# One shared block for four engines' loops, a branch hint marked in every turn, an evener spread of q, and a shorter early part of wo

## The chip, the cores and the metric

One core of one Trainium2 chip. The time is device microseconds (us) of one execution; times of a kernel are medians of several executions, with the lowest and highest where they matter. The profile is one such execution, and its span, from the first to the last instruction, is 1.3 to 1.6 us shorter than the time of the same run. No execution of any kernel was over 1.5% above the fastest of the same kernel, so all count as fast.

## The reference

One decode step of attention with grouped heads, gated by a small MLP. All tensors are bf16.

```python
def _A_ref(x, k_cache, v_cache, wq, wo):          # k_cache, v_cache: [2, 8, 32768, 128]
    q = (x @ wq).reshape(B, Sq, Hq, Dh).transpose(0, 2, 1, 3)      # Hq = 32, Dh = 128
    k = jnp.repeat(k_cache, rep, axis=1)                            # rep = 4
    v = jnp.repeat(v_cache, rep, axis=1)
    p = _softmax(jnp.einsum("bhqd,bhkd->bhqk", q, k) * (Dh ** -0.5), axis=-1)
    o = jnp.einsum("bhqk,bhkd->bhqd", p, v)
    return o.transpose(0, 2, 1, 3).reshape(B, Sq, Hq * Dh) @ wo
...
x = A_x                                            # [2, 1, 512]
xn = _layernorm(x, axis=-1)
s = _A_ref(xn, A_k_cache, A_v_cache, A_wq, A_wo)
g = _silu(_B_ref(xn, B_w1, B_w2, B_w3, B_w4))      # the MLP, 512 -> 512 -> 1792 -> 512
return x + s * g
```

There are 2 x 8 = 16 head groups, each with 8.39 MB of K and 8.39 MB of V, read once.

## The kernel before

SyncE issues all large loads in order. Each of the other engines runs a loop over the head groups, and they hand work on through semaphores. The parts that the change and the argument touch, with cuts marked:

```python
WO_PARTS = [(0, 0, 8), (0, 8, 16), (1, 0, 8), (1, 8, 12), (1, 12, 14), (1, 14, 15), (1, 15, 16)]
...
hint_p, hint_v = pe.mark_branch_hint_location(), dve.mark_branch_hint_location()   # at the program's start
...
wait(pool, k_qT, (g_, g_.n))                       # q is spread by 16 casts of GpSimd
for n in range(NQ):
    for j in range(NQ):
        G(spread(pool, j, n))
...
with act.Fori(0, NG):                              # NG = 16: ScalarE, exp of the scores
    ...
with pool.Fori(0, NG) as m:                        # GpSimd, places q for the next group
    ...
with dve.Fori(0, NG // 2) as t:                    # VectorE, two groups in a turn
    for odd in range(2):
        heads(oA[:, bass.ds(t * (2 * RS) + odd * RS, RS)], 0)   # closes the group before
        group(odd)                                              # transposes K, then the exponentials
...                                                # VectorE: copies and heads() of the last group
turn = pe.alloc_register("turn")                   # TensorE
pe.reg_mov(turn, 0)
nc.br("turn", engines=[pe.engine])
nc.switch_bb("turn")
loop = nc.cur_bb
head_sums()
pe.reg_add(turn, turn, 1)
pe.br_lt(turn, NG + 1, on_true="group", on_false="tail")
nc.switch_bb("group")
...                                                # the K and V products of one group
nc.br("turn", engines=[pe.engine])
nc.switch_bb("tail", parent=loop)
...                                                # the wo product; output by SyncE
sp.wait_ge(s_out, 16)
...
for eng, hint, reg in ((pe, hint_p, turn), (dve, hint_v, end)):
    eng.br_lt(reg, 1, on_true="more", on_false="end").branch_hint(hint)
nc.switch_bb("more")
pe.sem_inc(s_end, 1)
dve.sem_inc(s_end, 1)
nc.switch_bb("end", parent=tail)
```

The last branches are never taken. They exist so that a hint can be attached to them. In the program a hint names a branch that comes later. The trace has TensorE's hint once, at 1.53 us, for 0.04 us.

The softmax here doesn't subtract the row's maximum and nothing guards it: scores larger than these inputs give would overflow.

## Time and profile before

| | kernel before |
|---|---|
| time, median of 3 | 653.87 us (653.72 to 654.01) |
| span of the profiled run | 652.4 us |
| bytes read | 280.50 MB |
| DMA in the loop (52 to 610 us) | 434 GB/s, share 1.00 |
| busy: TensorE / VectorE | 58% / 58% |
| last row of wo landed | 649.43 us |
| output issued, end of span | 650.68, 652.42 us |

The time is that of one uninterrupted stream of loads, with about 3 us behind the last byte. The prediction shows the lines. Two views of the kernel before that it didn't show became important. The first is what SyncE waits for at the end (engine, line, what it waited for: us in total, times, longest):

```profile
SPq L648 <- DMA out_dram<-out: 1.0, 1, 1.0
```

The second is the time line where VectorE enters its loop (start, duration, instruction, and in brackets the idle time before it with its releaser):

```profile
37.15 0.68 DVE L427 TENSOR_TENSOR g_f<-T 32x512 f32<-32x512 f32 x1 [0.69 <-ACT T L425]
38.46 0.69 DVE L502 TENSOR_TENSOR ox<-ps,sel_t 128x512 f32<-128x512 f32 x1 [0.63 <-DVEq L46]
```

VectorE's first multiply inside the loop starts 0.63 us after its last instruction ahead of the loop.

### The profile page before, as it was taken

How to read it: one execution, taken by the hardware profiler on the slowest of the kernel's cores; microseconds unless marked ns; L12 is line 12 of the kernel's file. 1: busy time of each engine (PE TensorE's matmuls, PEld its weight loads, DVE VectorE, ACT ScalarE, POOL GpSimd, SP SyncE). 2: the span in 40 equal slices, each digit the busy share in tenths (PEclk: the TensorE clock that was granted, in tenths of full speed). 3: DMA queues.
4: the chain of work that ended last, by engine and by line, in shares of the span. 5: the costliest groups of instructions: out<-in, count | busy, mean ns of one | idle time of the engine just before them, and what ended most of it. 6: DMA issues, size and time to landing. Idle time of an engine off the chain costs nothing. (4 is left out here: it accounts for less than half of the span.)

```text
span 652.4 us, 6348 instructions
## 1 busy us (share of the span) xinstructions
PE 376.6 (58%) x2164; PEld 140.1 (21%) x2196; DVE 375.5 (58%) x430; ACT 49.4 (8%) x92; POOL 11.9 (2%) x45
## 2 busy tenths in 40 slices
PE   0758392673829458283854819376381946728674
PEld 0213131221213122021321203122130312203221
DVE  6368392754729365481945639285472927548671
ACT  1011010000101001010100101000010100101010
POOL 1200000000000000000000000000000000000000
PEclk9859688785978968597786969769596886959797
DMA  9989998999899989998999899989998999899997
GB/s 387 482 386 450 450 450 386 450 450 450 386 450 450 446 390 450 450 450 386 450 450 450 386 450 450 450 386 450 450 450 386 450 450 450 386 450 420 447 420 322
DMA packets 6509, 280.51 MB, mean 430 GB/s; under 512 B 746, under 2 KB 1004, under 8 KB 1260
## 3 DMA queue, kind: packets, MB, share of 16 engines
q1 hardware_dynamic: 6492, 280.50, 99.5%
q14 instruction: 1, 0.01, 0.0%
q10 hardware_dynamic: 16, 0.00, 0.0%
HBM read 280.50 MB, written 0.00 MB: 430 GB/s over the span
## 5 line engine op out<-in xcount | busy, mean ns | idle before, releaser
L566 PE MATMUL ps<-T,zeros 128*128 128x512 bf16 x992 | 276.5, 425 | 173.2 <-PEq L46 164.4
L486 DVE STREAM_TRANSPOSE T<-kbuf 128x1024 int32<-128x1024 int32 x256 | 291.2, 1207 | 116.5 <-DVEq L46 115.7
L566 PEld LDWEIGHTS ps<-T,zeros 128*128 128x128 bf16 x1024 | 98.8, 104 | 346.1 <-issue 267.8
L579 PE MATMUL ps<-vbuf,pt 128*16 128x512 bf16 x1024 | 71.3, 441 | 40.5 <-PEq L46 40.5
L502 DVE TENSOR_TENSOR ox<-ps,sel_t 128x512 f32<-128x512 f32 x17 | 11.8, 692 | 83.4 <-DVEq L46 83.4
L453 ACT ACT_TABLE_LOAD x16 | 20.5, 1283 | 445.5 <-ACTq L46 445.5
L579 PEld LDWEIGHTS ps<-vbuf,pt 128*16 128x16 bf16 x1024 | 29.8, 101 | 82.1 <-issue 65.2
L493 DVE STREAM_TRANSPOSE pt<-ep 128x512 bf16<-128x512 bf16 x32 | 22.1, 692 | 28.7 <-DVEq L46 28.7
L543 PE MATMUL ps<-ob,sel_h 128*128 128x129 f32 x34 | 9.0, 350 | 39.3 <-PEq L46 39.3
L453 ACT ACTIVATE ep<-ps 128x512 bf16<-128x512 f32 x32 | 19.1, 597 | 104.7 <-ACTq L46 104.5
L507 DVE TENSOR_REDUCE ob<-ox 128x128 f32<-128x512 f32 x17 | 17.3, 1018 | 2.5
L543 PEld LDWEIGHTS ps<-ob,sel_h 128*128 128x128 f32 x34 | 5.8, 212 | 47.5 <-issue 47.5
L463 POOL TENSOR_TENSOR zeros<-qr,sel_j 128x64 bf16<-128x64 f32 x16 | 4.7, 294 | 571.8 <-POOLq L46 571.8
L343 PE MATMUL ps<-kbuf,xT 128*2 128x512 bf16 x32 | 3.6, 623 | 15.1 <-DVE xT L300 15.1
L511 DVE RECIPROCAL rec<-ps 128x1 f32<-128x1 f32 (+1 forms) x17 | 2.9, 169 | 14.0 <-DVEq L46 14.0
L519 DVE TENSOR_REDUCE oA<-xm 128x128 f32 x16 | 5.9, 366 | 3.8 <-DVEq L46 3.8
L417 PE MATMUL ps<-vbuf,zeros 128*32 x12 | 7.0, 585 | 0.8 <-issue 0.3
L513 DVE SCALAR_TENSOR_TENSOR xm<-ps,rec,mask 128x128 f32<-128x128 f32 (+1 forms) x17 | 6.0, 351 | 2.5
L453 ACT ACTIVATION_READ_ACCUMULATOR ep<-ps 128x1 f32 x32 | 6.2, 194 | 0.0
L423 DVE TENSOR_TENSOR T<-T,ps 32x512 f32<-32x512 f32 x1 | 0.7, 674 | 8.7 <-PE ps L421 8.7
L359 POOL CAST qr<-qT 32x64 bf16<-32x64 f32 x16 | 4.6, 286 | 4.9 <-DVE qT L352 4.0
L343 PEld LDWEIGHTS ps<-kbuf,xT 128*2 128x2 bf16 x32 | 0.9, 113 | 16.8 <-DVE xT L300 15.1
(59 smaller groups left out, 45.1 us busy)
## 6 DMA issues: line engine op xcount, KB each, us to landing
vbuf<-in_A_v_cache_dram SPq DMA_DIRECT2D x4, 4096.0 KB, 26.1
kbuf<-in_A_k_cache_dram SPq DMA_DIRECT2D x2, 4096.0 KB, 22.4
kbuf<-in_A_wq_dram SPq DMA_DIRECT2D x1, 4096.0 KB, 12.3
vbuf<-in_B_w_dram SPq DMA_DIRECT2D x2, 1792.0 KB, 17.1
kbuf<-in_A_wo_dram SPq DMA_DIRECT2D x3, 1024.0 KB, 32.3
kbuf<-in_A_wo_dram SPq DMA_DIRECT2D x1, 512.0 KB, 35.0
kbuf<-in_A_wo_dram SPq DMA_DIRECT2D x1, 256.0 KB, 35.2
kbuf<-in_A_wo_dram SPq DMA_DIRECT2D x2, 128.0 KB, 35.0
```

The source lines that it names most:

```text
L417: pe.matmul(h2[0:32, :], lhsT=h_bf[:, bass.ds(f, 1), :].rearrange("p f c -> p (f c)"), rhs=w4v[:, bass.ds(f, 1), :].rearrange("p f d -> p ...
L453: act.activation(out=eps_[i][:, :], in_=sc[i][:, :], func=ACT.Exp, scale=inv_sqrt_dh, accum_out=rss[i][:, :]).then_inc(s_e, 1)
L463: pool.tensor_tensor(out=zw, in0=qr[:, :, :, bass.ds(m * rep, rep)].rearrange("p n e h -> p (n e) h").unsqueeze(2).to_broadcast([128, NB * ...
L486: dve.transpose(out=Ts[(NR * i + r) % T_BUFS][:, :].rearrange("p (b t k) -> p t b k", b=NB, t=RT), in_=kt[:, r * W:(r + 1) * W].rearrange( ...
L493: dve.transpose(out=pts[h][:, :, :].rearrange("p r (t h) -> p t r h", h=rep), in_=eps_[i][:, :].rearrange("p (t r h) -> p t r h", r=NR, h= ...
L502: dve.tensor_tensor(out=ox[:, :].rearrange("p (t d) -> p t d", t=VT), in0=o[:, :].rearrange("p (t d) -> p t d", t=VT), in1=sel_t[:, :].uns ...
L507: dve.tensor_reduce(out=ob[:, 0:Dh], in_=ox[:, :].rearrange("p (t d) -> p d t", t=VT), axis=AX.X, op=ALU.add).then_inc(s_ob, 1)
L513: dve.scalar_tensor_tensor(out=xm[p0:, :, :], in0=oT[p0:, 0:Dh].rearrange("p (w r) -> p w r", w=WL), scalar=rec[p0:, 0:1], in1=mask[p0:, : ...
L519: dve.tensor_reduce(out=dst, in_=xm[p0:, :, :].rearrange("p w r -> p r w"), axis=AX.X, op=ALU.add).then_inc(s_r, 1)
L543: mm = pe.matmul(oT, lhsT=sel_h[:, :, :, :].rearrange("p j h w -> p (j h w)"), rhs=ob[:, :], start=True, stop=True)
L566: mm = pe.matmul(sc2[:, bass.ds(i * 512, 512)], lhsT=z[:, nb, e, zc:zc + 128], rhs=Tb[:, nb, :, e], start=(r == 0 and nb == 0 and e == 0), ...
L579: mm = pe.matmul(o[32 * j:32 * j + VT * rep, :], lhsT=pts[h][:, r, a * VT * rep:(a + 1) * VT * rep], rhs=vt[:, u * VT:(u + 1) * VT, :].rea ...
```

## The change

It has four parts. (1) The loops of ScalarE, GpSimd, VectorE and TensorE no longer have blocks of their own: all four begin at one label, "turn". (2) TensorE's hint isn't marked at the start for a branch at the end any more; it is marked at the head of each turn, for the loop's own compare-and-branch, which replaces the unconditional one. (3) Six of GpSimd's sixteen casts that spread q go to VectorE (4) and ScalarE (2). (4) The early partial sums of wo end at row 11 and not at row 12. The intent is that the hint goes with the branch that is taken in every turn, and that the end gets a little shorter. Cut to its core (VectorE's closing statements, which only move behind TensorE's loop in the text, are left out):

```diff
-WO_PARTS = [(0, 0, 8), (0, 8, 16), (1, 0, 8), (1, 8, 12), (1, 12, 14), (1, 14, 15), (1, 15, 16)]
+WO_PARTS = [(0, 0, 8), (0, 8, 16), (1, 0, 8), (1, 8, 11), (1, 11, 14), (1, 14, 15), (1, 15, 16)]
...
-    hint_p, hint_v = pe.mark_branch_hint_location(), dve.mark_branch_hint_location()
+    hint_v = dve.mark_branch_hint_location()
...
+    wait(act, k_qT)
     wait(pool, k_qT, (g_, g_.n))
+    wait(dve, k_qT)
     for n in range(NQ):
         for j in range(NQ):
-            G(spread(pool, j, n))
+            if n == 0:
+                V(spread(dve, j, n))
+            elif n == 1 and j < 2:
+                A(spread(act, j, n))
+            else:
+                G(spread(pool, j, n))
...
-    with act.Fori(0, NG):
+    turn = {e: e.alloc_register("turn") for e in (pe, act, pool, dve)}
+    for e in turn:
+        e.reg_mov(turn[e], 0)
+    nc.br("turn", engines=[e.engine for e in turn])
+    nc.switch_bb("turn")
+    loop = nc.cur_bb
+
+    @contextmanager
+    def turns(e, n):
+        yield e.snap(turn[e], min_val=0, max_val=n - 1)
+        e.reg_add(turn[e], turn[e], 1)
+        e.br_lt(turn[e], n, on_true="turn", on_false="group")
+
+    with turns(act, NG):
...
-    with pool.Fori(0, NG) as m:
+    with turns(pool, NG) as m:
...
-    with dve.Fori(0, NG // 2) as t:
+    with turns(dve, NG // 2) as t:
...
-    turn = pe.alloc_register("turn")
-    pe.reg_mov(turn, 0)
-    nc.br("turn", engines=[pe.engine])
-    nc.switch_bb("turn")
-    loop = nc.cur_bb
+    hint_p = pe.mark_branch_hint_location()
     head_sums()
...
-    nc.br("turn", engines=[pe.engine])
+    pe.br_lt(turn[pe], NG + 1, on_true="turn", on_false="tail").branch_hint(hint_p)
     nc.switch_bb("tail", parent=loop)
...
-    for eng, hint, reg in ((pe, hint_p, turn), (dve, hint_v, end)):
-        eng.br_lt(reg, 1, on_true="more", on_false="end").branch_hint(hint)
+    dve.br_lt(end, 1, on_true="more", on_false="end").branch_hint(hint_v)
     nc.switch_bb("more")
-    pe.sem_inc(s_end, 1)
     dve.sem_inc(s_end, 1)
```

More of the change, by code (lines that the diff above doesn't have):

```diff
@@ L1 @@
-from contextlib import ExitStack
+from contextlib import ExitStack, contextmanager
 import concourse.bass as bass
@@ L358, in spread @@
     def spread(eng, j, n):
-        return eng.tensor_copy(
+        return (eng.copy if eng is act else eng.tensor_copy)(
             out=qr[32 * j:32 * j + 32, :, :, :].rearrange("p a e (m n h) -> p (a e) m n h", n=NQ, h=rep)[
@@ L443 @@
         d_wo[i].after(sp.dma_start(out=wo3[:, g, w], in_=wos[:, g, w]), 16)
-    with act.Fori(0, NG):
+    wait(pool, (g_, g_.n), (v_, v_.n), (a_, a_.n))
+    pool.sem_inc(s_zf, 1)
+    wait(dve, (v_, v_.n), (g_, g_.n), k_x4)
+    dve.sem_inc(s_o, 1)
+    dve.sem_inc(s_tf, T_BUFS - 1)
+    dve.sem_inc(s_tl, 1)
+    turn = {e: e.alloc_register("turn") for e in (pe, act, pool, dve)}
[10 more added lines that the diff above has]
+    with turns(act, NG):
         for i in range(NPART):
@@ L458 @@
     zw = z[:, :, :, (NR - 1) * rep:].rearrange("p n e (j w) -> p (n e) j w", j=NQ)[:, :, :, 0:rep]
-    wait(pool, (g_, g_.n), (v_, v_.n), (a_, a_.n))
-    pool.sem_inc(s_zf, 1)
-    with pool.Fori(0, NG) as m:
+    with turns(pool, NG) as m:
         take(pool, s_zf)
@@ L521, in heads @@
             ).then_inc(s_r, 1)
-    wait(dve, (v_, v_.n), (g_, g_.n), k_x4)
-    dve.sem_inc(s_o, 1)
-    dve.sem_inc(s_tf, T_BUFS - 1)
-    dve.sem_inc(s_tl, 1)
-    with dve.Fori(0, NG // 2) as t:
+    with turns(dve, NG // 2) as t:
         for odd in range(2):
@@ L530 @@
             group(odd)
-    oA4 = oA[:, RS:].rearrange("p (b s j r) -> p j (b s) r", b=B, s=NS, j=NQ)
-    oX4 = oX[:, :].rearrange("p (s r) -> p s r", r=RS)
-    for j in range(NQ):
-        n = B * NS if j < NQ - 1 else B * NS - 1
-        w = slice(32 * j, 32 * j + 32)
-        i_c = dve.tensor_copy(out=oX4[w, 0:n, :], in_=oA4[w, j, 0:n, :])
-    i_c.then_inc(s_r, 1)
-    heads(oX4[32 * (NQ - 1):, B * NS - 1, :], 32 * (NQ - 1))
     def head_sums():
@@ L546, in head_sums @@
         mm.then_inc(s_x, 1)
-    turn = pe.alloc_register("turn")
-    pe.reg_mov(turn, 0)
-    nc.br("turn", engines=[pe.engine])
-    nc.switch_bb("turn")
-    loop = nc.cur_bb
+    hint_p = pe.mark_branch_hint_location()
     head_sums()
-    pe.reg_add(turn, turn, 1)
-    pe.br_lt(turn, NG + 1, on_true="group", on_false="tail")
+    pe.reg_add(turn[pe], turn[pe], 1)
+    pe.br_lt(turn[pe], NG + 1, on_true="group", on_false="tail")
     nc.switch_bb("group")
@@ L586 @@
     mm.then_inc(s_o, 1)
-    nc.br("turn", engines=[pe.engine])
+    pe.br_lt(turn[pe], NG + 1, on_true="turn", on_false="tail").branch_hint(hint_p)
     nc.switch_bb("tail", parent=loop)
+    oA4 = oA[:, RS:].rearrange("p (b s j r) -> p j (b s) r", b=B, s=NS, j=NQ)
+    oX4 = oX[:, :].rearrange("p (s r) -> p s r", r=RS)
+    for j in range(NQ):
+        n = B * NS if j < NQ - 1 else B * NS - 1
+        w = slice(32 * j, 32 * j + 32)
+        i_c = dve.tensor_copy(out=oX4[w, 0:n, :], in_=oA4[w, j, 0:n, :])
+    i_c.then_inc(s_r, 1)
+    heads(oX4[32 * (NQ - 1):, B * NS - 1, :], 32 * (NQ - 1))
     step = NS * RS // BS
@@ L648 @@
     sp.wait_ge(s_out, 16)
-    tail, s_end = nc.cur_bb, nc.alloc_semaphore("s_end")
-    end = dve.alloc_register("end")
+    tail, end, s_end = nc.cur_bb, dve.alloc_register("end"), nc.alloc_semaphore("s_end")
     dve.reg_mov(end, 1)
-    for eng, hint, reg in ((pe, hint_p, turn), (dve, hint_v, end)):
-        eng.br_lt(reg, 1, on_true="more", on_false="end").branch_hint(hint)
+    dve.br_lt(end, 1, on_true="more", on_false="end").branch_hint(hint_v)
     nc.switch_bb("more")
-    pe.sem_inc(s_end, 1)
     dve.sem_inc(s_end, 1)
```

## The prediction

> **What bounds the kernel now.** I read the page's table of DMA queues first, then a table of stretches, then the waits, then the end of the program in order of time. The queues come first because the kernel has only 280.5 MB to bring in and the engines' shares are low (TensorE and VectorE 58% each).
>
> ```profile
> q1 hardware_dynamic: 6492, 280.50, 99.5%
> q14 instruction: 1, 0.01, 0.0%
> HBM read 280.50 MB, written 0.00 MB: 430 GB/s over the span
> ```
>
> The columns of the first two lines are packets, MB and share of 16 engines' span. The data queue is busy for all of the span but its very ends, and exactly one packet of instructions was fetched while the kernel ran. Next the stretches: the loop, the last head group with the first rows of wo, and what follows the last byte of wo.
>
> ```profile
> core 0: us, PE busy (x) PEld busy (x) DVE busy (x) ACT busy (x) POOL busy (x), PEclk, DMA share, GB/s
> 52.00:610.00 558.00, 324.93 (x1896) 122.41 (x1923) 321.92 (x351) 39.89 (x75) 4.41 (x15) 0.80 1.00 434
> ...
> 640.00:649.10 9.10, 6.83 (x70) 2.23 (x62) 2.61 (x5) 0.27 (x1) 0.00 (x0) 0.69 0.96 394
> 649.10:652.40 3.30, 0.62 (x20) 0.35 (x16) 0.58 (x2) 0.31 (x1) 0.00 (x0) 1.00 0.00 1
> ```
>
> In the loop DMA runs at share 1.00 and 434 GB/s while every compute engine has 40% of its time free. (The digits 386 and 450 that alternate on the page are packets falling into slices; stretches of hundreds of us give 434.) The waits say the same from VectorE's side:
>
> ```profile
> DVE T L486 <- DVEq L46: 115.7, 15, 9.4
> ```
>
> That is us in total, times, longest. VectorE, which begins each head group by transposing K, waits 115.7/15 = 7.7 us in every turn after the first, until K has landed. The loads themselves are ahead: one 8.39 MB load takes 8.39 MB / 434 GB/s = 19.3 us, and the page has a median of 27.2 us from issue to landing of K, so a load stands 7.9 us in the queue before its bytes move. Both numbers say that a turn of the loop has about 7.7 us of slack. So only the two ends can move the time: about 1 us ahead of the first packet, and what follows the landing of wo. That end, in order of time:
>
> ```profile
> 648.16 0.10 PEld L604 LDWEIGHTS ps<-kbuf,zeros 128*17 128x17 bf16 x4 [0.85 <-DMA kbuf<-in_A_wo_dram]
> 648.17 0.61 PE L604 MATMUL ps<-kbuf,zeros 128*17 128x512 bf16 x4
> 648.80 0.12 PEld L616 LDWEIGHTS ps<-kbuf,zeros 128*17 128x17 bf16 x8 [0.53 <-DMA kbuf<-in_A_wo_dram]
> 648.80 0.40 PE L616 MATMUL ps<-kbuf,zeros 128*17 128x128 bf16 x8
> 648.83 0.59 ACT L629 COPY T<-ps 128x512 f32<-128x512 f32 x1 [16.95 <-PE ps L604]
> 649.46 0.13 PEld L633 LDWEIGHTS ps<-T,zeros 128*17 128x17 f32 x8 [0.54 <-ACT T L629]
> 649.47 0.41 PE L633 MATMUL ps<-T,zeros 128*17 128x128 f32 x8 [0.27 <-ACT T L629]
> ```
>
> Each line is start, duration, instruction, and in brackets the idle time before it with what ended it. The last four rows of the early sums (L604, rows 8 to 11 of the second half of wo) waited for DMA. ScalarE's copy of the sums followed at once, and TensorE sat idle 0.27 us before it could add the copied sums (L633). Products of rows 14 and 15 (8 matmuls, L616), two VectorE instructions of 0.29 us and the output transfer close the program.
>
> [...]The trace shows no such stall in this loop: one instruction packet in 652 us, and TensorE's first weight load of a new turn (L543, at 570.46) stands 0.12 us after the VectorE reduce that it waits for (569.32 + 1.02 = 570.34). [...]the four of L604 took 0.61 us together, and their median alone is 0.631 us.
>
> **The change part by part.**
>
> *One block for the loops of ScalarE, GpSimd, VectorE and TensorE.* Comparing the built programs, the instructions within each engine's loop are the same in number and order, apart from TensorE's. Loop counters and branches are as many. Nothing is on the path: 0 us.
>
> *TensorE's hint and branch.* Out: one hint at the program's start, a never-taken branch at its very end, an unconditional branch per turn. In: one hint per turn and a compare-and-branch in place of the unconditional one. [...]In each turn it lies where TensorE waits for two VectorE operations (0.69 + 1.02 us), so it is hidden even from the turn, and the turn has 7.7 us spare: 0 us. In the last turn, too, the hint runs while TensorE waits for the last reduce.
>
> *Spreading q.* Six of GpSimd's sixteen casts (0.286 us each, L359) move: four to VectorE, two to ScalarE. GpSimd is done 1.7 us earlier (near 23.6 us instead of 25.3), but its next instruction (L463) starts at 39.78 because it waits for other engines' counts. VectorE has 3.20 us idle from 19.76 before L388; four casts at an estimated 0.3 us fit. ScalarE is idle for 12.64 us there. 0 us.
>
> *Partial sums end at row 11.* Parts of 4 and 2 rows become 3 and 3. A row is 128 KB, so the fourth part ends 131072 B / 434 GB/s = 0.30 us earlier. From the issue times (613.08, 613.55, 614.02, 614.50) plus 35.0, 35.2, 35.1 and 34.9 us the parts land at 648.1, 648.75, 649.1 and 649.4; the fourth will land at 647.8. TensorE must also be free: batches of four 512-column matmuls at half clock (0.50 there) start about 0.43 us apart, and the previous one starts at 647.56, so the last batch of early sums can start at 648.0 instead of 648.17. Being three side by side and not four, it still takes 0.61 us. The copy then runs from about 648.65 to 649.24 instead of 648.83 to 649.42. The fifth part, now rows 11 to 13, lands at 648.75 as before, but has 12 matmuls: 8 took 0.40 us, of which one batch of four is about 0.13, so 12 take about 0.53: 648.80 to 649.33. Now TensorE, not the copy, is what the 8 matmuls of L633 wait for: 649.33 instead of 649.47. The last products need row 15, at 649.4; they come at about 649.45 to 649.55, just behind it. Gain: 0.14 us.
>
> Sum: 653.87 - 0.14 = 653.73 us; I say 653.7.
>
> **The rivals.**
>
> 1. *The hint now does harm at the exit.* [...]the code behind the loop is reached by a taken branch at the end of the last turn[...]. If that code must be fetched behind the full data queue, the stall lies wholly on the end. For the size: a 2 KB transfer issued on the ScalarE queue at 1.96 us landed at 8.2 us, so up to 6 us, giving 655 to 660. For it: the old hint stood there for something. Against: [...]before the change the exit showed 0.07 us (645.49 to 645.56).
>
> 2. [...]
>
> 3. *The gain of the row cut vanishes.* If the landing of row 15 or the matmuls of the longer fifth part end up last, the 0.14 us shrink to 0: 653.9. Or TensorE is back at full clock earlier and it becomes 0.3: 653.55.
>
> 4. *A stall per turn.* Anything below 7.7 us per turn is absorbed by the slack; only above that would it reach the time, 16-fold. Nothing points to it.
>
> **Range and chances.** The three runs of before lie 0.29 us apart, and the end offers at most the time between row 15's landing (649.4) and the end of the last product (650.0), 0.6 us: low 653.2. The upper end takes in rival 2 in part and the spread: 654.3. Rival 1 gets some 5% and remains within 2% (13 us) anyway. A gain of 13 us would need fewer bytes or more than 434 GB/s: chance 0.005. A loss of 13 us would need a stall of 8.5 us (7.7 + 13/16) in each turn: 0.01.
>
> **What would show each step right or wrong.** Right: 434 GB/s in the loop, VectorE's wait for K still near 7.7 us per turn, one instruction packet or so, the copy of the sums starting about 0.2 us earlier relative to the landing of the last rows, and no idle of TensorE before L633's counterpart. Wrong: more instruction packets than a few, a gap of over 0.3 us between the last head-sum matmul and the first wo product, a wait of the K transposes that has shrunk by microseconds, or an idle before the last products put down to the wo transfer. The time itself would refute me if it left 653.2 to 654.3, most likely upward through the exit.

The step of TensorE's hint stood at 0 us, and the sum is 653.87 - 0.14 = 653.73 us, with the row cut as its only term that isn't 0. 0 us stands as the author's estimate; the records of the kernel after have 0.04 us for a hint and 0.21 us for the branch, beside the 0.69 + 1.02 us that TensorE waits in each turn. "No such stall" in the text is a stall of TensorE at the loop's own branch. The 0.3 us for a cast on VectorE is an estimate; its four took 1.14 us together in the kernel after, 0.26 us each.

## The result, and the profile after

| | before | after |
|---|---|---|
| median, 6 runs each, same chip | 653.94 us (653.6 to 654.79) | 654.73 us (654.57 to 654.88) |
| span of the profiled run | 652.42 us | 653.54 us |
| last row of wo landed | 649.43 us | 649.76 us |
| from there to the issue of the output | 1.25 us | 1.37 us |
| from the issue of the output to the end | 1.74 us | 2.41 us |

The ratio is 1.001, with a 95% interval of 0.9998 to 1.0023. The interval takes in 1, so the times of this batch alone don't show that the kernel became slower; the spans further below do. Here and below a ratio is the mean time of one kernel's fast runs over that of the other's of the same rounds, so it is not quite the ratio of the medians quoted. "Within 2%" was right. The time is 1.0 us above the predicted 653.7 and 0.4 us above the upper end of the range.

The last three rows of the table add up the difference of the spans: 0.33 + 0.12 + 0.67 = 1.12 us. So the stream ended later, and the output took longer. The table of queues of the kernel after says what was in the way (packets, MB, share):

```profile
q1 hardware_dynamic: 6492, 280.50, 99.3%
q14 instruction: 2, 0.02, 0.0%
...
HBM read 280.50 MB, written 0.00 MB: 429 GB/s over the span
```

The same 6492 data packets and 280.50 MB, but two instruction packets instead of one, and a slightly lower share of the data queue. In the stretches (columns as in the prediction) the loop is what it was:

```profile
52.00:610.00 558.00, 330.12 (x1928) 121.35 (x1925) 321.90 (x349) 39.87 (x75) 4.38 (x15) 0.80 1.00 434
640.00:649.10 9.10, 6.49 (x61) 1.98 (x61) 2.61 (x5) 0.14 (x1) 0.00 (x0) 0.70 0.98 406
649.10:652.40 3.30, 1.31 (x28) 0.69 (x28) 0.58 (x2) 0.45 (x1) 0.00 (x0) 0.50 0.02 6
```

434 GB/s again; what changed is in the last stretch, where 6 GB/s now move instead of 1. VectorE's wait for K is unchanged too:

```profile
DVE T L511 <- DVEq L46: 115.4, 16, 9.3
```

It was 115.7 us. So no stall per turn has appeared. Looking at the transfers of 650 to 655 us alone, first in the kernel before, then in the kernel after:

```profile
DMA packets 12, 0.00 MB, mean 0 GB/s; under 512 B 12, under 2 KB 12, under 8 KB 12
...
q1 hardware_dynamic: 12, 0.00, 0.2%
```

```profile
DMA packets 13, 0.01 MB, mean 2 GB/s; under 512 B 12, under 2 KB 12, under 8 KB 12
...
q14 instruction: 1, 0.01, 0.6%
```

The twelve packets are the output. In the kernel after an instruction packet lies among them. The DMA records of the trace put it at 652.12 us, with 8192 bytes and 495 ns; nine of the output's packets lie at 652.40 to 652.45 us, the other three at 652.61 to 652.64 us, just behind it. In the kernel before all twelve lie at 651.96 to 652.04 us. SyncE's wait shows the effect:

```profile
SPq L666 <- DMA out_dram<-out: 1.7, 1, 1.7
```

1.7 us for 1.0 us. The other packet is at 41.89 us (8192 bytes, 309 ns), where the stream already runs. The packet of the kernel before was at 606.00 us and is gone. The end of the program in order of time, to be held against the seven lines in the prediction:

```profile
647.46 1.46 PE L622 MATMUL ps<-kbuf,zeros 128*17 128x512 bf16 x11 [0.20 <-DVE zeros L544]
...
648.96 0.58 ACT L647 COPY T<-ps 128x512 f32<-128x512 f32 x1 [16.86 <-PE ps L622]
...
649.13 0.50 PE L634 MATMUL ps<-kbuf,zeros 128*17 128x128 bf16 x12 [0.21 <-DMA kbuf<-in_A_wo_dram]
649.60 0.15 PEld L651 LDWEIGHTS ps<-T,zeros 128*17 128x17 f32 x8 [0.25 <-ACT T L647]
649.60 0.63 PE L651 MATMUL ps<-T,zeros 128*17 128x128 f32 x8
...
650.01 0.44 PE L634 MATMUL ps<-kbuf,zeros 128*17 128x128 bf16 x8
650.49 0.29 DVE L659 TENSOR_TENSOR sg<-ps,g 113x128 f32<-113x128 f32 x1 [3.08 <-PE ps L634]
```

TensorE adds the copied sums (L651) with no idle time before it, where it had been idle for 0.27 us. The copy starts 0.80 us ahead of the landing of the last row (649.76 - 648.96); it had been 0.60 us (649.43 - 648.83).

One more difference stood at the entry of VectorE's loop:

```profile
36.04 0.68 DVE L434 TENSOR_TENSOR g_f<-T 32x512 f32<-32x512 f32 x1 [0.69 <-ACT T L432]
38.37 0.69 DVE L527 TENSOR_TENSOR ox<-ps,sel_t 128x512 f32<-128x512 f32 x1 [1.64 <-DVEq L46]
```

The idle time is 1.64 us and no longer 0.63. Nothing waits for those 1.0 us, since the stream sets the pace (434 GB/s, share 1.00), but they are a mark.

### The profile page after: what moved, and what is told of

Its sections match the earlier page's. It is cut to its first block, busy times and chain, and to the rows that moved or that the text cites. A ratio compares the mean times of both kernels' runs of the same rounds, so it can differ in the third digit from the quotient of the medians.

```text
span 653.5 us, 6401 instructions
## 1 busy us (share of the span) xinstructions
PE 382.5 (59%) x2199; PEld 138.5 (21%) x2199; DVE 376.5 (58%) x434; ACT 50.0 (8%) x94; POOL 10.2 (2%) x39
## 3 DMA queue, kind: packets, MB, share of 16 engines
q1 hardware_dynamic: 6492, 280.50, 99.3%
HBM read 280.50 MB, written 0.00 MB: 429 GB/s over the span
## 5 line engine op out<-in xcount | busy, mean ns | idle before, releaser
L574 PE MATMUL ps<-T,zeros 128*128 128x512 bf16 x1024 | 280.5, 424 | 168.5 <-PEq L46 163.5
L511 DVE STREAM_TRANSPOSE T<-kbuf 128x1024 int32<-128x1024 int32 x256 | 291.3, 1207 | 115.8 <-DVEq L46 115.4
L587 PE MATMUL ps<-vbuf,pt 128*16 128x512 bf16 x1024 | 74.6, 456 | 38.8 <-PEq L46 38.8
L269 DVE MEMSET ps<- 128x4096 f32 x1 | 3.5, 3472 | 0.9 <-issue 0.9
```

The costliest lines, as they stand in the source:

```text
L511: dve.transpose(out=Ts[(NR * i + r) % T_BUFS][:, :].rearrange("p (b t k) -> p t b k", b=NB, t=RT), in_=kt[:, r * W:(r + 1) * W].rearrange( ...
L574: mm = pe.matmul(sc2[:, bass.ds(i * 512, 512)], lhsT=z[:, nb, e, zc:zc + 128], rhs=Tb[:, nb, :, e], start=(r == 0 and nb == 0 and e == 0), ...
L587: mm = pe.matmul(o[32 * j:32 * j + VT * rep, :], lhsT=pts[h][:, r, a * VT * rep:(a + 1) * VT * rep], rhs=vt[:, u * VT:(u + 1) * VT, :].rea ...
```

## The experiments

The kernel before ran as well; its medians in the five batches below were 654.05, 654.45, 654.25, 654.67 and 654.21 us, with single runs from 653.2 to 655.7. So a difference of some tenths between batches is scatter, and I lean on the packets and waits, which hardly vary, ahead of the times. (The medians of its spans are 652.5, 652.7, 652.6, 652.6 and 652.7 us, so most of this scatter lies outside the span.) The texts speak of these theories. Theory 1: the packet under the output is VectorE's, whose program got longer by four casts. Rival A: the change of TensorE's hint causes the packets. Theory 2 and Rival D, formed after the first batch: what costs is that no hint stands through the whole run (2), or the hint in each turn makes both 8 KB packets itself (D). Theory 3, formed after the second: each packet sets one of the sixteen DMA engines back, and a hint that stands from start to end spares TensorE's. Theory J, formed after the fourth: the packets are VectorE's, and it takes the shared block and the hint together. All of these are suppositions that the runs were to test. "Armed" in those texts means that a hint has been executed; whether it then stays in force, or is used up when its branch runs, is supposition too, and no run shows such a state. Packets are told below with the time, queue and size that the DMA records show; packets ahead of the span's start, which every run has, are left out.

### One part at a time: spread, hint, row

a_spread_back is the kernel after with all casts on GpSimd again; b_spread is the kernel before with only the casts moved; a_hint_back is the kernel after with TensorE's hint and branches as before, shared block kept; a_wo_back is the kernel after with row 12.

```diff
 # a_spread_back, to after          (b_spread: the reverse, to before)
-            if n == 0:
-                V(spread(dve, j, n))
-            elif n == 1 and j < 2:
-                A(spread(act, j, n))
-            else:
-                G(spread(pool, j, n))
+            G(spread(pool, j, n))
 # a_hint_back, to after
+    hint_p, hint_v = pe.mark_branch_hint_location(), dve.mark_branch_hint_location()   # at the start
-    hint_p = pe.mark_branch_hint_location()                                            # in the turn
-    pe.br_lt(turn[pe], NG + 1, on_true="turn", on_false="tail").branch_hint(hint_p)
+    nc.br("turn", engines=[pe.engine])
+    ...                                             # and the never-taken branch at the end
 # a_wo_back, to after
-WO_PARTS = [... (1, 8, 11), (1, 11, 14), ...]
+WO_PARTS = [... (1, 8, 12), (1, 12, 14), ...]
```

> The changed kernel with all sixteen casts of q back on GpSimd. Theory 1 (VectorE's program grew by the four casts and their wait[...]): the instruction packet at 652.1 us is gone, the wait for the output transfer falls from 1.7 to about 1.0 us, the time falls by 0.6 to 0.8 us to about 654.0. Rival A (the fetch is TensorE's, because its hint for the program's end is gone): packet and 1.7 us stay, time stays near 654.7. Rival B (the row cut costs): time stays near 654.7. Rival C (only the data stream is slower in some runs): packet stays, time anywhere in 653.6 to 654.8.

> The kernel before with only the casts of q spread over three engines. Theory 1: an instruction packet appears after 651 us, the wait for the output rises from 1.0 to about 1.7 us, time rises by 0.6 to 0.8 us over the kernel before. Rival A and rival B: no late packet, time within 0.2 us of the kernel before.

> The changed kernel with TensorE's hint and branches as before (one hint at the start for a branch at the very end, unconditional back branch). Theory 1: the late instruction packet and the 1.7 us wait for the output stay, time near 654.7. Rival A: packet gone, wait 1.0 us, time about 654.0. Rival B: no difference, 654.7.

> The changed kernel with the partial sums ending at row 12 again. Theory 1 and rival A: packet and 1.7 us stay; by my step for the row cut the time rises by 0.1 to 0.2 us, to about 654.9. Rival B: time falls by 0.5 us or more, to 654.2 or less.

| run | median us | ratio to before [95%] | instruction packets | SyncE's wait for the output |
|---|---|---|---|---|
| a_spread_back | 654.83 | 1.0015 [1.0002, 1.0029] | 42.0, 607.1, 652.1 (8 KB each, queue 14) | 1.7 |
| b_spread | 653.85 | 0.9995 [0.9982, 1.0009] | none | 1.0 |
| a_hint_back | 653.52 | 0.9992 [0.9979, 1.0006] | none | 1.0 |
| a_wo_back | 654.99 | 1.0012 [0.9998, 1.0026] | 42.1, 652.4 (8 KB, queue 14) | 2.0 |

Theory 1 fell: with the casts back on GpSimd both new packets stayed, and with the casts moved in the kernel before none came. What the casts do is to remove the packet at 606 us, which is there in the four kernels with GpSimd's program at its longer length (before, b_wo11, a_spread_back and, below, a_start_poolpad). Of Rival A the packets and the time came: with the hint back at the start both packets are gone and the time is 1.2 us shorter. Its reason, that the fetch is TensorE's because the hint for the program's end is gone, did not last: a_no_hint, below, lacks that hint too and has neither packet. The row cut is worth what little was expected: 0.26 us between a_wo_back and after, within the scatter.

### Which property of the hint

Four kernels, all with the shared block. a_no_hint has no hint of TensorE at all. a_hint_start has the hint at the start for the branch at the end, with the new compare-and-branch in the loop. a_hint_tail has the same hint marked only behind the loop. a_end_unhinted has the branch at the end and no hint for it.

```diff
 # all four, to after
-    hint_p = pe.mark_branch_hint_location()                                            # in the turn
-    pe.br_lt(turn[pe], NG + 1, on_true="turn", on_false="tail").branch_hint(hint_p)
+    pe.br_lt(turn[pe], NG + 1, on_true="turn", on_false="tail")
 # a_hint_start also                                  (a_hint_tail: marked after switch_bb("tail"))
+    hint_p, hint_v = pe.mark_branch_hint_location(), dve.mark_branch_hint_location()   # at the start
+    pe.br_lt(turn[pe], 1, on_true="more", on_false="end").branch_hint(hint_p)          # at the end
 # a_end_unhinted also
+    pe.br_lt(turn[pe], 1, on_true="more", on_false="end")
```

> The changed kernel with TensorE's hint of every turn left out and nothing in its place. Theory 2 (what costs is the absence of a hint that stands armed through the whole run; the hint of every turn does nothing): instruction packets at about 42 and 652 us as in the changed kernel, wait for the output 1.7 us, time near 654.7. Rival D (the hint of every turn itself causes the packets): both packets gone, wait 1.0 us, time near 653.6.

> The changed kernel with the hint at the program's start for a never-taken branch at its end, and the compare-and-branch of every turn without a hint. Theory 2 and rival D: no packet in the run, wait for the output 1.0 us, time near 653.5. Rival E (the compare-and-branch at the loop's end in place of an unconditional branch is what costs): packets and 654.7 us stay.

> As the run before this one, but with the hint placed behind the loop, at the head of the last block. It tells the two packets apart. Theory 2: the packet at 42 us stays, the one at 652 us is gone or comes near 647 us, wait for the output 1.0 us, time between the two, about 654.0 to 654.2: the difference from a hint at the start is the price of the packet at 42 us[...], the difference from no hint the price of the late one (0.5 to 0.7 us). Rival D: no packet at all, 653.5.

> The changed kernel without any hint on TensorE, but with the never-taken branch at the program's end. Theory 2: the branch alone does nothing, packets at 42 and 652 us stay, time near 654.7. Rival F (the branch at the end, not the hint, spares the fetch): the packet at 652 us is gone, the wait for the output 1.0 us, time 654.0 or less.

| run | median us | ratio to before [95%] | instruction packets | wait for the output |
|---|---|---|---|---|
| a_no_hint | 654.61 | 1.0003 [0.999, 1.0017] | 68.6 (16 KB, queue 8) | 1.0 |
| a_hint_start | 653.54 | 0.9986 [0.9972, 0.9999] | none | 1.0 |
| a_hint_tail | 654.98 | 1.0007 [0.9993, 1.002] | 68.4 (16 KB, queue 8) | 1.0 |
| a_end_unhinted | 654.63 | 1.0003 [0.9989, 1.0017] | 68.5 (16 KB, queue 8) | 1.0 |

Without the hint in the turn both 8 KB packets are gone, as Rival D had it, and Theory 2 fell. Rival E fell too: a_hint_start has the compare-and-branch and no packet. So did Rival F: a_no_hint has no branch at the end, and the packet at 652 us is gone there as well. Yet the time hardly fell, because another packet has come: 16384 bytes on queue 8, while the loop runs. The transfers of 68 to 70 us in a_no_hint:

```profile
q1 hardware_dynamic: 16, 1.05, 122.7%
q8 instruction: 1, 0.02, 2.9%
```

The DMA records give it 931 ns. It matters for the whole stream, as the landings of the loads show. In us, as differences to b_turn_hint (a run without any packet, below):

| load landed at (b_turn_hint) | after | a_spread_back | before | a_no_hint |
|---|---|---|---|---|
| 39.98 | +0.36 | +0.06 | +0.21 | +0.18 |
| 49.65 | +0.80 | +0.91 | +0.21 | +0.19 |
| 59.30 | +0.80 | +0.91 | +0.20 | +0.17 |
| 78.62 | +0.77 | +0.90 | +0.19 | +1.51 |
| 600.23 | +0.89 | +0.81 | +0.33 | +1.38 |
| 609.91 | +0.88 | +0.82 | +0.68 | +1.41 |
| 638.96 (last of V) | +0.88 | +0.81 | +0.63 | +1.39 |

The packet at 42 us moves the landings by 0.4 us in one step and in a_spread_back by 0.85 us, the packet of before at 606 us by 0.35, and the 16 KB packet by 1.3. A packet of 8 KB is 0.02 us of 434 GB/s. Why the loss is so much larger can be read from the records of landings, of which the table gives only the last of each load. Each load lands in sixteen pieces, and it is complete with the last. A packet holds back one piece: in a_spread_back the last piece lands 0.02 us after the last but one at 39.98, and 0.85 us after it at 49.65, while the middle of the sixteen doesn't move. In a_no_hint the last piece is 1.34 us behind from 78.62 on. This also explains why the packet at 607 us in a_spread_back adds nothing (0.81 to 0.82): it sets another piece back, so that the last but one is 0.71 us ahead of the last at 600.23 and 0.19 us at 609.91, and the load still waits for the last one. That the piece belongs to one DMA engine is an inference, since the records don't name the engine.

Two cautions. A lag shrinks a little over the run (a_no_hint: 1.34 us at 78.62 and 1.16 us at the end of wo). And not every shift is a packet's: between 117 and 253 us all sixteen pieces of a_dve_own, a kernel without any packet (below), fall another 0.3 to 0.5 us behind those of b_turn_hint, and the middle of the pieces of the kernel after does so by 0.4 us. So the last rows of the table hold to about half a microsecond; the steps at the packets are sharper.

So there is an instruction packet near 68 us, on the face of it TensorE's, since only its hint differs, and a hint at the start spares it. a_hint_tail and a_end_unhinted say that the branch at the end isn't what does it: of the three kernels with that branch, only a_hint_start, with the hint for it marked ahead of the loop, has no packet at 68 us.

### Casts, row, and the pad

b_wo11 is the kernel before with row 11 alone, b_spread_wo11 with row 11 and the casts (so it is a_hint_back less the shared block). a_start_poolpad is a_hint_start with six idle semaphore counts on GpSimd ahead of its loop, to lengthen its program again. a_hint_once is the kernel after with the hint for the loop's branch marked once ahead of the loop, not in each turn.

```diff
 # a_start_poolpad, to a_hint_start
+    s_pad = nc.alloc_semaphore("s_pad")
+    for _ in range(6):
+        pool.sem_inc(s_pad, 1)
 # a_hint_once, to after
+    hint_p = pe.mark_branch_hint_location()      # before nc.br("turn", ...)
-    hint_p = pe.mark_branch_hint_location()      # in the turn
```

> The kernel before with the row cut alone. My step of the prediction: 0.14 us less than before, the packet near 606 us as before, wait for the output 1.0 us, time near 653.8. Rival B (the row cut costs): 654.2 or more, and longer than before by the end of the program in the profile.

> The kernel before with the spread casts and the row cut, but its own loops, blocks and hint: the changed kernel with the hint back, less the shared block. Theory 3 (each instruction packet that runs beside the stream sets one of the sixteen DMA engines back and costs 0.3 to 1.3 us of the end; a hint that stands armed from start to end spares TensorE's; nothing else in the change but the row cut counts): no packet, last V half lands near 639.1 us, wait for the output 1.0 us, time near 653.5, 0.5 us under the kernel before. Rival G (the shared block itself brought part of the gain of the run with the hint back): 653.8 or more.

> The changed kernel with the hint at the start and six idle semaphore instructions added to GpSimd ahead of its loop, which makes its program as long as before. Theory 3: an 8 KB packet returns near 606 us, the landings after it come 0.3 us later, the time rises from 653.5 to about 653.8. Rival H (the packet at 606 us is not a matter of GpSimd's length, or costs nothing): no packet, or 653.5 all the same.

> The changed kernel with the hint for the loop's own branch armed once, ahead of the loop, instead of in every turn. Theory 3, with the hint used up when its branch first runs near 68 us: the packet at 42 us stays (it follows the first arming), the late one at 652 us is gone or replaced by the 16 KB packet near 68 us, wait for the output 1.0 us, time 654.2 to 654.8. Rival I (the hint is not used up): like the changed kernel, both packets, wait 1.7 us, 654.7.

| run | median us | ratio to before [95%] | instruction packets | wait for the output |
|---|---|---|---|---|
| b_wo11 | 653.91 | 0.9998 [0.9985, 1.0012] | 605.6 (8 KB, queue 14) | 1.0 |
| b_spread_wo11 | 653.74 | 0.9991 [0.9978, 1.0005] | none | 1.0 |
| a_start_poolpad | 653.57 | 0.9988 [0.9974, 1.0001] | 605.8 (8 KB, queue 14) | 1.0 |
| a_hint_once | 655.43 | 1.0017 [1.0004, 1.0031] | 41.9, 652.7 (8 KB, queue 14), 107.2 (16 KB, queue 8) | 1.7 |

The pad brought the packet at 606 us back, so on this evidence it is GpSimd's and follows the length of its program. Its landings step by 0.28 us, but only 0.1 to 0.2 us of it was left at the end and the median didn't show it. Row 11 alone is 653.91 against 654.25 of before in the same batch (spans: 652.5 for 652.6), no more than scatter. b_spread_wo11 and a_hint_back differ in the shared block alone and lie 0.2 us apart: the block by itself costs nothing. a_hint_once keeps both 8 KB packets although the hint is executed once, so "in each turn" isn't what matters. It has the 16 KB packet as well, at 107 us, with a step of 0.6 us, and it is the slowest of all.

### Is it the hint of the last turn?

a_turn_then_end is the kernel after with a second hint, marked behind the loop, for a branch at the end, so that the loop's hint isn't the last one executed. a_hint_group marks the hint at the head of the block "group", behind the branch that leaves the loop, so that it isn't executed in the last turn.

```diff
 # a_turn_then_end, to after
     nc.switch_bb("tail", parent=loop)
+    hint_e = pe.mark_branch_hint_location()
+    ...                                             # pe.br_lt(..., on_true="more", on_false="end").branch_hint(hint_e)
 # a_hint_group, to after
-    hint_p = pe.mark_branch_hint_location()         # in "turn"
     nc.switch_bb("group")
+    hint_p = pe.mark_branch_hint_location()
```

> The changed kernel with its hint of every turn, and behind the loop a second hint for a never-taken branch at the program's end. If the late packet comes from a hint left armed at the exit, the second hint takes its place: packet at 42 us stays, none at 652 us, wait for the output 1.0 us, time near 654.0. If the late packet needs only that a hint was armed in the loop: both packets, 1.7 us, 654.7.

> The changed kernel with the hint moved behind the branch that can leave the loop, so that every arming is followed by its branch and none is left at the exit. If the late packet comes from a hint left armed: packet at 42 us stays, none at 652 us (perhaps the 16 KB packet near 68 us, since no hint stands between two turns), wait 1.0 us, 654.0, or 654.6 with that packet. If not: both packets, 1.7 us, 654.7.

| run | median us | ratio to before [95%] | instruction packets | wait for the output |
|---|---|---|---|---|
| a_turn_then_end | 654.65 | 1.0005 [0.9992, 1.0019] | 41.8, 651.9 (8 KB, queue 14), 648.7, 651.8 (16 KB, queue 8) | 1.6 |
| a_hint_group | 655.10 | 1.0008 [0.9994, 1.0021] | 40.9, 652.5 (8 KB, queue 14), 648.7 (16 KB, queue 8) | 1.7 |

That theory fell: the late 8 KB packet stays in both. But the two showed something else. The packets that are new in them, at 648.7 and 651.8 us, are of 16 KB and on queue 8, like the one near 68 us; those at 42 and 652 us are of 8 KB and on queue 14, like GpSimd's. They need not be TensorE's at all. And all kernels that have them (after, a_spread_back, a_wo_back, a_hint_once, a_turn_then_end, a_hint_group) have a hint that names the label "turn" where VectorE's loop begins too.

### The fourth corner, and VectorE alone outside the block

b_turn_hint is b_spread_wo11 (every engine with its own loop) with TensorE's hint in each turn as in the kernel after. a_dve_own is the kernel after with VectorE's loop alone taken out of the shared block.

```diff
 # b_turn_hint, to b_spread_wo11
-    hint_p, hint_v = pe.mark_branch_hint_location(), dve.mark_branch_hint_location()
+    hint_v = dve.mark_branch_hint_location()
+    hint_p = pe.mark_branch_hint_location()         # in the turn
     head_sums()
-    nc.br("turn", engines=[pe.engine])
+    pe.br_lt(turn, NG + 1, on_true="turn", on_false="tail").branch_hint(hint_p)
-    ...                                             # TensorE's branch at the end
 # a_dve_own, to after
-    turn = {e: e.alloc_register("turn") for e in (pe, act, pool, dve)}
+    turn = {e: e.alloc_register("turn") for e in (pe, act, pool)}
-    with turns(dve, NG // 2) as t:                  # the loop and its helpers also stand ahead of
+    with dve.Fori(0, NG // 2) as t:                 # nc.br("turn", ...) in the text
```

> Own loops of every engine as in the kernel before (with the spread and row 11), but TensorE's hint armed in each turn as in the kernel after: the fourth corner of shared block or not, hint in the turn or at the start. Theory J (the 8 KB packets at 42 and 652 us are VectorE's: with one shared block the hint's target is also the head of VectorE's loop[...]): VectorE's first multiply of the loop waits about 0.63 us for its branch as before, not 1.64; no 8 KB packet at 42 or 652 us; SyncE's wait for the output 1.0 us; time 653.6, or up to 654.3 if TensorE fetches 16 KB somewhere. Rival D as it stood (the hint in each turn makes both packets by itself, block shared or not): both packets stay, the wait is 1.7 us, time 654.7.

> The kernel after with VectorE's loop taken out of the shared block (its own loop again), TensorE, ScalarE and GpSimd still sharing, hint in each turn. Theory J: the same as b_turn_hint, no 8 KB packets at 42 and 652 us, VectorE's gap 0.63 us, wait for the output 1.0 us, time 653.6 (up to 654.3 with a 16 KB packet of TensorE). Rival D: packets stay, 1.7 us, 654.7. If b_turn_hint is clean and this one is not, it is the block as such (ScalarE or GpSimd) and not VectorE's place in it.

| run | median us | ratio to before [95%] | instruction packets | wait for the output |
|---|---|---|---|---|
| b_turn_hint | 653.37 (652.95 to 653.5) | 0.9983 [0.9969, 0.9996] | none | 1.0 |
| a_dve_own | 653.65 (653.11 to 653.89) | 0.9984 [0.997, 0.9998] | none | 1.0 |

Both are clean. SyncE's wait and VectorE's entry into its loop in a_dve_own:

```profile
SPq L666 <- DMA out_dram<-out: 1.0, 1, 1.0
```

```profile
37.11 0.69 DVE L489 TENSOR_TENSOR ox<-ps,sel_t 128x512 f32<-128x512 f32 x1 [0.63 <-DVEq L46]
```

And the same two views in b_turn_hint:

```profile
SPq L656 <- DMA out_dram<-out: 1.0, 1, 1.0
```

```profile
37.48 0.69 DVE L509 TENSOR_TENSOR ox<-ps,sel_t 128x512 f32<-128x512 f32 x1 [0.63 <-DVEq L46]
```

The wait is 1.0 us and the gap 0.63 us, as before. The transfers of 650 to 655 us in a_dve_own are the output's twelve packets alone:

```profile
DMA packets 12, 0.00 MB, mean 0 GB/s; under 512 B 12, under 2 KB 12, under 8 KB 12
```

Rival D in its own form fell: a hint in each turn with loops of their own brings no packet, and has the lowest median. What Theory J forecast came true in both. The four corners, all with the casts moved and row 11:

| | TensorE's hint at the start, for the branch at the end | TensorE's hint in each turn, for the loop's branch |
|---|---|---|
| every engine its own loop | b_spread_wo11 653.74, no packets | b_turn_hint 653.37, no packets |
| one shared block | a_hint_back 653.52, no packets | after 654.73, packets at 42 and 652 us |
| shared, but not by VectorE | | a_dve_own 653.65, no packets |

The spans of all executions say the same: 653.2 us or more in every kernel with the pair, 652.6 us or less in every kernel without a packet.

| instruction packets | kernels | median span, us |
|---|---|---|
| none | b_spread, b_spread_wo11, b_turn_hint, a_hint_back, a_hint_start, a_dve_own | 652.0 to 652.4 |
| at 606 us | before, b_wo11, a_start_poolpad | 652.2 to 652.7 |
| 16 KB near 68 us | a_no_hint, a_hint_tail, a_end_unhinted | 653.3 to 653.6 |
| 42 and 652 us, others or not | after, a_spread_back, a_wo_back, a_turn_then_end, a_hint_group | 653.3 to 653.7 |
| 42, 107 and 652 us | a_hint_once | 654.1 |

In the profiles the time from the issue of the output to the end is 2.36 to 2.67 us in the six kernels with the late packet and 1.72 to 1.74 us in the other twelve.

Neither the block nor the hint costs anything by itself. Only both together do, and it is enough to take VectorE out of the block. a_dve_own and the kernel after differ in the place of VectorE's loop alone, and their spans by 653.54 - 652.56 = 0.98 us: 0.28 us in the landing of the last row of wo (649.76 and 649.48), 0.01 us from there to the output's issue, 0.69 us from there to the end (2.41 and 1.72). The 0.69 is firm. The 0.28 is not: the profiled execution of a_dve_own is the slowest of its five and has the shift of 0.5 us told above. In the six kernels without a packet the last row lands at 648.91 to 649.48 us, in the five with the pair and no 16 KB packet within the loop at 649.48 to 649.82; the medians are 0.6 us apart.

What stays open. The trace doesn't name the engine that a packet was fetched for, nor where the code lies in memory; that the packets are VectorE's rests on the comparison just made and on the gap at its loop's entry, which is 1.64 us (1.83 in a_spread_back) in the six kernels with the pair and 0.63 us in the other twelve. Six of these have VectorE in the shared block; in a_hint_start it is the same line as in the kernel after:

```profile
37.87 0.69 DVE L527 TENSOR_TENSOR ox<-ps,sel_t 128x512 f32<-128x512 f32 x1 [0.63 <-DVEq L46]
```

The late packet starts 1.1 us after VectorE's last branch in all six, but also 1.0 us after SyncE's issue of the output, so its place doesn't tell the two apart. Why a hint for the shared label brings VectorE's gap to 1.64 us from 0.63, I could not see, and nothing here shows it. And of the 0.7 us under the output, only some 0.15 us are seen in the packets (the last one 0.24 us after the first and not 0.08 us); SyncE then notices the end 0.9 us after the last packet, where it took 0.4 us.

## Why the prediction was wrong, by its steps

**What bounds the kernel.** Right: 434 GB/s in the loop before and after, and VectorE's wait for K 115.4 us for 115.7. The medians of all kernels lie between 653.3 and 655.5 us.

**One block for the loops: 0 us.** Right by itself (b_spread_wo11 and a_hint_back, 0.2 us apart), wrong in company. I compared the instructions within each engine's loop and found them the same; which instruction packets come isn't in that comparison.

**TensorE's hint and branch: 0 us.** This is the step that failed. It counted sequencer time in TensorE and showed it to be hidden, and it was: VectorE's wait for K has not changed (115.4 us for 115.7). The records have 0.04 us for a hint and 0.21 us for the new branch back, where the old one took 0.18. (It is 0.21 us without the hint as well, in a_hint_start, so nothing here shows that the hint made its branch quicker.) What the step left out is that a changed hint can change which instruction packets come while the data queue is full and the output is under way. Together with the shared block it put one 8 KB packet into the stream at 42 us and one under the output at 652 us. In the profile that is 0.28 + 0.69 = 0.97 us (the kernel after against a_dve_own), 1.1 us in the medians of both times and spans (653.4 and 652.3 us). It also rated the old hint too low. I wrote that it "stood there for something", and then priced its removal at nothing; the three kernels in which no hint stands before or in the loop pay 1.3 us for a 16 KB packet at 68 us.

**Spreading q: 0 us.** Nearly right. GpSimd and VectorE had the room (VectorE's four casts took 1.14 us, where it had 3.20 us idle before). Not foreseen: GpSimd's shorter program loses the packet at 606 us, worth 0.35 us of the stream; b_spread is 0.2 us faster than before in its batch.

**Partial sums end at row 11: -0.14 us.** The mechanism was right. The copy starts 0.2 us earlier relative to the last landing, TensorE no longer waits for it, and the twelve matmuls took 0.50 us where I had 0.53. In the times it is 0.3 us (b_wo11) and 0.26 us (a_wo_back), in the spans 0.1 and 0.2 us, all within the scatter. In the profile of the kernel after it is hidden by TensorE's clock, 0.50 in the last stretch for 1.00 before, so that the last products took longer. b_spread_wo11 had a clock of 0.99 from 649.1 to 650.5 us and took 1.10 us from the last landing to the issue of the output, 0.15 less than before.

**The rivals.** Rival 1 had the right place, the end, and the right culprit, the hint, and the wrong victim: it looked for a stall of TensorE as it leaves the loop, up to 6 us. There is none: from the last head-sum matmul to the first wo product it is 0.07 us (646.06 to 646.13), as before. The packet hit the output's transfer. A packet in each turn didn't come; there were two in all, and each cost far more than its bytes over the bandwidth (0.02 us): the landings step by 0.4 us at the first, and the wait for the output is 0.7 us longer with the second. Rival 3 came in part: from the last landing to the issue of the output the kernel after took 1.37 us for 1.25, so none of the 0.14 us is left there, though for the clock and not for the causes that the rival named. Rival 4 didn't come.

**The range.** I built its upper end from the scatter of before and part of Rival 2, so with that rival cut the upper end is no more than my estimate. "One instruction packet or so" was on my list of signs that all is well; I had not asked what a single packet is worth. The profile of before could have told: its half loads there land 9.67 us apart, but 10.03 us apart (600.56 to 610.59) across the packet at 606 us.

## What to carry to other kernels

Where the load stream is the bound, as here at 434 GB/s, an instruction packet can move its landings: count the instruction packets, find when each comes, and look whether the landings step there; here one packet moved the landings by up to 1.3 us, by nothing where another piece of the load was later still, and one under the output's transfer cost 0.7 us. A branch hint or a shared label should be judged by the instruction packets that come with it and by the gaps of all engines that have code at the label (here two 8 KB packets and a gap of 1.64 us for 0.63), and not by the sequencer time of the hint (0.04 us). A kernel to keep is b_turn_hint, with the hint in each turn, the casts spread, row 11, and loops of their own: 653.37 us, a ratio of 0.9983 to before, and 1.4 us below the kernel after in the medians. a_hint_back has the same median span (652.0 us), so the runs don't rank the kernels without packets.
